# Two of eight list maxima placed between dependent folds in a top-k attention kernel

## Chip, cores and metric

The kernel runs on one core of a Trainium2 chip. The metric is the time of one execution in microseconds of the device; the median of three runs of the kernel before is 854.37 us (853.60 to 854.74). The profile is one further execution with a span of 853.3 us.

## The reference

Attention that keeps, in each row of scores, only those not below the row's 32nd largest, followed by a highway layer on the result. Cut to what matters:

```python
# q, k, v: (8, 8, 576, 64) float32
scores = scale * np.matmul(q, k.transpose(0, 1, 3, 2))          # 576 scores a row
kth = np.partition(scores, -32, axis=-1)[..., -32:-32 + 1]
scores = np.where(scores >= kth, scores, -1000000000.0)
attn = np.exp(scores - scores.max(axis=-1, keepdims=True))
x = (attn / (attn.sum(axis=-1, keepdims=True) + 1e-09)) @ v     # to (4608, 512)
H = np.maximum(x @ w_h, 0.0)
T = 1.0 / (1.0 + np.exp(-(x @ w_t + b_t)))
out = T * H + (1.0 - T) * x
```

## The kernel before

A *tile* is 128 query rows of one head (or 64 rows of two heads). Two tiles make a *pair*, the unit of a step; two pairs make a *quad*. There are 144 steps and 72 quads, numbered from 0. A *group* is the set of pairs that share the same rows of one batch: four pairs, or two for the remainder of 64 rows.

**How the 32nd largest value of a row is found.** Sorting 576 values on VectorE in rounds of eight would be long, so the row is first split into lists by pairwise maxima and minima:

- `tree` (L250), once in a step: `hi` holds the larger of score i and score i + 288, for two tiles of the quad. It reads the scores in PSUM (`ps`) and ScalarE's copy in SBUF (`z`, written by `evac`, L239). As soon as it ends, PE may overwrite the single PSUM tile `ps` with the next pair's scores.
- `folds` (L267), once a quad, at odd steps, for all four tiles at once: `hh` is the larger of the halves of `hi` (144 values a tile), `h3` the larger of the halves of `hh` (72), and a third operation puts the smaller of those halves into columns 72 to 143 of the list `w2`. Each of the first two reads what the instruction in front of it wrote; the third reads `hh`.
- `minima` (L287) on POOL: with integer additions it turns `hh` and `hi`, in place, into the smaller ones of their pairs. It is made to wait for the last fold of the quad.
- `tops` (L312), a generator for each tile: largest eight of `h3`, strike them out, next eight, strike them out, then the largest eight of each half of the small `hh`. That is six steps of one VectorE operation each (a strike-out shows in the trace as two rows, a load of the values and the replacement).
- `rest` (L333), a generator for each tile: largest eight of the small `hi`, then the last rounds over the 168 collected values; it ends with the threshold `m4`.

VectorE's maximum of eight is MAX8 in the trace. `run` (L389) advances a list of generators in turn, one step of each a round, so that neighbouring instructions belong to different tiles:

```python
    def run(gens, rounds=99):
        while gens and rounds:
            gens[:] = [x for x in gens if next(x, 0) is None]
            rounds -= 1
```

**Order.** Engines are fed in the order of the program (`keep_in_program_order`, L35), so the order below is also that of each queue. In step n the loop at L974 issues: the tree of pair n; at odd n the folds and POOL's minima of quad n // 2 (L979); masks and the product with the values of earlier pairs on ScalarE and PE; the scores and `evac` of pair n + 1; pieces of the highway layer. Then come VectorE's lists. At odd n `rest` for the first two tiles of quad n // 2 - 1 and two rounds of `rest` for its other two (L1032). At even n the end of those two, and then all of `tops` for the four tiles of quad n // 2 - 1, in rounds; a group that has ended puts a reciprocal (`norm`) behind the second round:

```python
                    gens = ops.lists(n - 2, *pairs[n - 2]) if have(n - 2) else []
                    ops.run(gens, 2)
                if ended:
                    ops.norm(pairs[n - 5][0])
                ops.run(gens)
```

So VectorE ends an even step with eight MAX8 on `hh` of the older quad (two rounds over four tiles), and begins the odd step with tree, `hh`, `h3` and the third fold of the newer one. `settle` (L394), on POOL, subtracts the lists' ends from the threshold once a group is done.

In the profile every instruction of the main loop has the line L35, which records it, so it is told by its tiles: `hi<-ps,z` is the tree, `hh<-hi` the first fold, `h<-hh` the second, `w<-hh` as TENSOR_TENSOR the third and as MAX8 a list maximum.

Of the kernel before, what the change touches and what calls it, by code (L numbers as in the profile page):

```python
# [67 lines left out]
class Ops:  # L68
# [195 lines left out]
            hi[:, half, :], ps[:, :, 0:H1], sc[:, :, H1:S], ALU.max  # L264
        )

    def folds(self, k, g, pi):  # L267


        vec, P, S, H = self.nc.vector, self.P, self.S, self.H  # L270
        H1, H2, H3 = S // 2, S // 4, S // 8
        if pi == 0:
            g.w2 = self.lpool.tile([P, H, H2 + 32], FP32, tag="w2", name="w2")
        hi, hh, h3 = self.quads[k]
        vec.tensor_tensor(hh[:], hi[:, :, 0:H2], hi[:, :, H2:H1], ALU.max)
        a, b = hh[:, :, 0:H3], hh[:, :, H3:H2]
        vec.tensor_tensor(h3[:], a, b, ALU.max)
        last = vec.tensor_tensor(
            g.w2[:, 2 * pi : 2 * pi + 4, H3:H2], a, b, ALU.min
        )  # L280
        if k == 0:
            last = vec.tensor_tensor(
                hh[:], hi[:, :, 0:H2], hi[:, :, H2:H1], ALU.min
            )
        return last
# [478 lines left out]
def kernel(  # L764
# [65 lines left out]
    with ExitStack() as cm:  # L830
        ops = Ops(cm, tc, shared, exact=False)

        def load_weights():
            for src, dst in ((moe_w_h, wh), (moe_w_t, wt)):
                ops.nc.gpsimd.dma_start(
                    dst[:], src.rearrange("(g p) n -> p g n", p=P)
                )
            bt_bcast = bass.AP(
                tensor=moe_b_t.tensor, offset=moe_b_t.offset, ap=[[0, P], [1, dm]]
            )  # L840
            ops.nc.gpsimd.dma_start(bt[:], bt_bcast)
# [7 lines left out]
        def out_rows(g):  # L849
            if not g.rem:  # L850
                r0 = g.b * S + g.qt
                return [out[r0 : r0 + JP : J, :]]
            ends = [(g.b + i) * S for i in (0, 1)]
            return [out[r1 - R : r1, :] for r1 in ends]
# [10 lines left out]
        pairs = [(g, pi) for g in groups for pi in range(len(g.pairs))]  # L865
# [36 lines left out]
        def have(n):  # L902
            return 0 <= n < NPR
# [57 lines left out]
            vec.tensor_reduce(flag_f[:], bps[0:1, 0:P], op=ALU.max, axis=AX.X)  # L961
            vec.tensor_copy(flag[:], flag_f[:])

        late = []
        def attend(m):
            ops.mask(m, *pairs[m])
            values(m - 1)
            ops.trans(m)

        def values(m):  # L970
            g, pi = pairs[m]
            ops.av(m, g, pi, preps[g.b]["vb"])

        while step <= NPR:  # L974
            n = step
            if have(n):
                ops.tree(n)
                if n % 2:
                    ops.minima(n // 2, ops.folds(n // 2, *pairs[n - 1]))  # L979
                if n + 2 < NHP:  # L980
                    ops.turn(pr, "kin", n + 2, True)
                if NHP <= n + 1 < 2 * NHP:
                    ops.turn(pr, "qin", n + 1 - NHP, None, 1)
                if n == NHP:
                    ops.load(pr, "qin", 3, None, None, 1)
                if n == 2 * NHP:
                    ops.turn_rest(pr, 0, NHP, ("qrest",))
            if n == 5:
                load_weights()
            if have(n - 4):  # L990
                ops.mask(n - 4, *pairs[n - 4], tis=(0,))
            kind = fg = None
            nextg = None
            if ffn and (ffn[0][0] != "x" or n % 2):
                kind, fg = ffn.pop(0)
                if kind == "t" and ffn and ffn[0][0] == "x":
                    nextg = ffn.pop(0)[1]
            if have(n - 5):
                values(n - 5)
            if have(n - 4):  # L1000
                ops.mask(n - 4, *pairs[n - 4], tis=(1,))
            if have(n + 1):
                g, pi = pairs[n + 1]
                ops.scores(n + 1, g, pi, preps[g.b])
                ops.evac(n + 1)
            if kind == "x":
                ops.ffn_x(fg)
            if kind == "h":
                ops.ffn_h(fg)
                ops.ffn_r(fg)  # L1010
                ops.ffn_d(fg)
            if kind == "t":
                ops.ffn_t(fg)
                ops.ffn_e(fg)
                ops.ffn_o(fg, *out_rows(fg))
            if n == 3:
                ops.values_rest(pr)
                ops.values(pr, 0)
            if n == 4:
                ops.values(pr, 1)  # L1020
            ended = False
            if have(n - 5):
                g, pi = pairs[n - 5]
                ended = pi == len(g.pairs) - 1 and (not g.rem or g.r0 > 0)
            if n % 2:
                gens = ops.lists_rest(n // 2 - 1, *pairs[n - 3]) if have(n - 3) else []
                late = gens[2:]
                gens = gens[0:2]
                if n == 1:
                    opening = ops.lists(0, *pairs[0])  # L1030
                    ops.run(opening, 2)
                ops.run(gens)  # L1032
                ops.run(late, 2)
            else:
                ops.run(late)
                if n == 2:
                    gens = opening
                else:
                    gens = ops.lists(n - 2, *pairs[n - 2]) if have(n - 2) else []
                    ops.run(gens, 2)  # L1040
                if ended:
                    ops.norm(pairs[n - 5][0])
                ops.run(gens)
            if nextg:
                ops.ffn_x(nextg)
            if have(n - 4):
                ops.trans(n - 4)
            if ended and not pairs[n - 5][0].last:
                ops.norm_heads(pairs[n - 5][0])
            for piece in pieces.pop(n, []):  # L1050
                piece()
            if n % 2 == 0 and have(n - 3):
                g, pi = pairs[n - 3]
                if pi == len(g.pairs) - 1:
                    ops.settle(g)
            if ended:
                g = pairs[n - 5][0]
                ffn += [("x", g), ("h", g), ("t", g)]
            step += 1
# [13 lines left out]
        late = ops.lists_rest(m // 2 + 1, *pairs[m + 1])  # L1073
        gens, late = late[0:2], late[2:]
# [49 lines left out]
    with tc.If(taken > 0):  # L1124
        with tc.For_i(0, B, 1) as b:
            with ExitStack() as cm:
                ops = Ops(cm, tc, shared, exact=True)
# [17 lines left out]
                n = 0  # L1145
                for qt in range(nck):
                    g = Group(b, qt, 0, H, P)
# [49 lines left out]
```

## Time and profile before

| | |
|---|---|
| median of three runs | 854.37 us |
| span of the profiled execution | 853.3 us |
| VectorE (DVE) busy | 823.3 us, 96% |
| ScalarE (ACT) busy | 762.4 us, 89% |
| GpSimd (POOL) busy | 710.4 us, 83% |
| TensorE (PE) busy | 706.0 us, 83% |
| tree: count, median | 142, 737 ns |
| fold `hh`: count, median | 73, 758 ns |
| fold `h3`: count, median | 72, 457 ns |
| third fold: count, median | 72, 451 ns |
| MAX8 on `hh` (72 values): count, median | 576, 217 ns |

[...] neighbours on one engine can overlap, so starts, and not durations, add up to the span. Busy time counts an overlap once. The trees of the first two pairs and one more fold of quad 0 have forms of their own.

### The profile page before, as it was taken

To read this page: it belongs to the slowest core of one execution; us is meant where nothing else is said; L and a number is where in the kernel's file an instruction comes from. 1 tells how busy PE (TensorE), PEld (TensorE's weight loads), DVE (VectorE), ACT (ScalarE), POOL (GpSimd) and SP (SyncE) were. 2 spreads that over 40 slices of the span, in tenths; PEclk is the share of its full clock that TensorE was granted. 3 is DMA by queue.
4 is the path that set the end of the run, shared out by engine and by line. 5 is a ranking of instruction groups with operands and counts; after the bars stand their busy time and mean duration, and the time that the engine had idled before them with its cause. 6 is when DMAs were issued, how large, how long until landed. Compare 5 with 4: busy or idle time off the path is not lost.

```text
span 853.3 us, 20051 instructions
## 1 busy us (share of the span) xinstructions
PE 706.0 (83%) x6520; PEld 492.0 (58%) x6566; DVE 823.3 (96%) x4168; ACT 762.4 (89%) x1523; POOL 710.4 (83%) x457
## 2 busy tenths in 40 slices
PE   7788888888888888888888888879888888887865
PEld 4565555565566555565556555656556665555543
DVE  4999999999999999999999999999999999999994
ACT  3799998899999999799999999989999999889974
POOL 5788888888889889878889888888888988887991
PEclk9699999999999999999999999999999999999998
DMA  8463413234244331433325342323413211111311
GB/s 187 126 114 69 112 33 68 51 70 99 38 90 91 75 88 27 74 70 63 88 51 94 64 108 41 63 50 69 112 39 68 49 34 28 39 38 26 47 33 38
DMA packets 105184, 58.12 MB, mean 68 GB/s; under 512 B 82288, under 2 KB 91888, under 8 KB 105072
## 3 DMA queue, kind: packets, MB, share of 16 engines
q1 hardware_dynamic: 93200, 37.47, 17.1%
q0 software_dynamic: 11056, 19.01, 15.7%
q8 instruction: 53, 0.87, 0.4%
q14 instruction: 59, 0.48, 0.2%
q10 hardware_dynamic: 816, 0.30, 0.1%
HBM read 30.67 MB, written 18.35 MB: 57 GB/s over the span
## 4 chain that ended last, share of the span: by engine, by line
DVE 92%; PE 3%; ACT 2%; POOL 1%; issue 1%; DVEq 0%; POOLq 0%; ACTq 0%
DVE w L35 50%; DVE m L35 19%; DVE hi L35 11%; DVE hh L35 7%; DVE h L35 4%; PE ps L35 1%; ACT pen L35 1%; ACT et L35 1%; PE t L35 1%; PE kqps L35 0%; DVE scales L35 0%; PE zt L35 0%; ACT z L35 0%; POOL hh L35 0%; PE warm L35 0%
## 5 line engine op out<-in xcount | busy, mean ns | idle before, releaser
L35 PE MATMUL ps<-kq 64*128 64x64 f32 (+3 forms) x1280 | 210.6, 453 | 65.4 <-DVE hi L35 62.6
L35 ACT ACTIVATE pen<-z,m 128x576 bf16<-128x576 f32 x288 | 226.7, 788 | 0.2
L35 PE MATMUL zt<-ident,z 128*128 128x128 f32 x1152 | 217.3, 282 | 5.5 <-ACT xT L35 5.5
L35 ACT ACTIVATE z<-ps 128x1152 f32<-128x1152 f32 x144 | 162.9, 1131 | 58.7 <-PE ps L35 56.2
L35 PE MATMUL zt<-nident,pen 128*128 128x128 bf16 x1152 | 207.5, 221 | 0.1
L35 PEld LDWEIGHTS ps<-kq 64*128 64x128 f32 (+1 forms) x1280 | 106.7, 182 | 164.2 <-issue 83.6
L35 POOL TENSOR_TENSOR hi<-z,hi 128x1152 int32<-128x1152 int32 x72 | 189.3, 2629 | 13.9 <-DVE m L35 8.3
L35 POOL TENSOR_TENSOR hi<-hi,z 128x1152 int32<-128x1152 int32 x72 | 190.5, 2646 | 5.6
L35 PEld LDWEIGHTS zt<-ident,z 128*128 128x128 f32 x1152 | 164.4, 143 | 21.4 <-ACT xT L35 6.4
L35 POOL TENSOR_TENSOR hh<-hi,hh 128x576 int32<-128x576 int32 x71 | 104.0, 1465 | 87.2 <-DVE w L35 87.2
L35 ACT ACTIVATE et<-zt 128x512 bf16<-128x512 f32 x288 | 163.6, 601 | 9.4 <-PE zt L35 4.9
L35 PEld LDWEIGHTS <-pen 128*128 128x128 bf16 x1440 | 152.8, 107 | 14.4 <-ACT pen L35 9.1
L35 DVE MAX8 m<-w 128x8 f32<-128x168 f32 x576 | 159.7, 318 | 0.0
L35 PE MATMUL zr<-v,et 128*128 128x65 bf16 (+1 forms) x1590 | 98.3, 196 | 45.4 <-ACT et L35 38.1
L35 PEld LDWEIGHTS <-et 128*128 128x128 bf16 (+1 forms) x1600 | 69.2, 101 | 84.2 <-ACT et L35 81.7
L35 DVE MAX8 w<-hi 128x8 f32<-128x288 f32 x288 | 116.1, 444 | 0.0
L35 DVE TENSOR_TENSOR hi<-ps,z 128x576 f32<-128x576 f32 x142 | 104.7, 737 | 1.3 <-ACT z L35 1.2
L35 POOL TENSOR_TENSOR hh<-hh,hi 128x576 int32<-128x576 int32 x71 | 100.2, 1411 | 5.6
L35 DVE MATCH_REPLACE8 w<-m,w 128x168 f32<-128x168 f32 x288 | 89.0, 316 | 0.0
L35 DVE MAX8 w<-hh 128x8 f32<-128x72 f32 x576 | 84.0, 217 | 0.0
L35 PE MATMUL zr<-ident,z 128*128 128x128 f32 x286 | 68.9, 294 | 6.0 <-ACT xs L35 5.9
L35 ACT ACTIVATE x<-xs,scales 128x64 f32<-128x64 f32 x272 | 68.2, 336 | 0.0
(96 smaller groups left out, 1154.3 us busy)
## 6 DMA issues: line engine op xcount, KB each, us to landing
x<-d POOLq DMA_DIRECT2D x34, 256.0 KB, 3.9
vin<-in_v_dram SPq DMA_DIRECT2D x8, 1024.0 KB, 5.6
kin<-in_k_dram SPq DMA_DIRECT2D x63, 128.0 KB, 3.2
out_dram<-d SPq DMA_DIRECT2D x30, 256.0 KB, 2.2
out_dram<-t POOLq DMA_DIRECT2D x30, 256.0 KB, 4.1
qin<-in_q_dram SPq DMA_DIRECT2D x56, 128.0 KB, 3.0
qrest<-in_q_dram SPq DMA_DIRECT2D x8, 128.0 KB, 4.1
vrest<-in_v_dram SPq DMA_DIRECT2D x8, 128.0 KB, 2.9
```

Of the source, the lines that this page charges most:

```text
L35: return self._tc.keep_in_program_order(fn(*args, **kw))
```

## The change

`folds` is given a list of up to two generators. It advances the first to its end ahead of the fold `hh` and the second ahead of the fold `h3`. At even steps the loop runs `tops` for three more rounds, after which each of the four tiles has one MAX8 left; those of the first two tiles follow as before, and those of the other two are kept in `fill` for the folds of the next step. In the last step, which no folds follow, all four run at once.

```diff
-    def folds(self, k, g, pi):
+    def folds(self, k, g, pi, fill):
...
         hi, hh, h3 = self.quads[k]
+        self.run(fill[0:1])
         vec.tensor_tensor(hh[:], hi[:, :, 0:H2], hi[:, :, H2:H1], ALU.max)
+        self.run(fill[1:2])
         a, b = hh[:, :, 0:H3], hh[:, :, H3:H2]
         vec.tensor_tensor(h3[:], a, b, ALU.max)
...
-        late = []
+        late, fill = [], []
...
                 if n % 2:
-                    ops.minima(n // 2, ops.folds(n // 2, *pairs[n - 1]))
+                    ops.minima(n // 2, ops.folds(n // 2, *pairs[n - 1], fill))
+                    fill = []
...
                 if ended:
                     ops.norm(pairs[n - 5][0])
+                ops.run(gens, 3)
+                if have(n + 1):
+                    gens, fill = gens[0:2], gens[2:4]
                 ops.run(gens)
```

## The prediction

> **What bounds the kernel now.** I read the page's shares first, then the windows, then the chain of waits. In the first fence (the page) the busy shares leave VectorE ahead, and the chain runs over it for nine tenths of the span.
>
> ```profile
> span 853.3 us, 20051 instructions
> ...
> PE 706.0 (83%) x6520; PEld 492.0 (58%) x6566; DVE 823.3 (96%) x4168; ACT 762.4 (89%) x1523; POOL 710.4 (83%) x457
> ...
> DVE 92%; PE 3%; ACT 2%; POOL 1%; issue 1%; DVEq 0%; POOLq 0%; ACTq 0%
> ```
>
> 96% is an average over a start and a tail in which VectorE has little to do. The windows view (each engine's busy time in a stretch) for the middle of the run has:
>
> ```profile
> 63.00:700.00 637.00, 538.79 (x5056) 377.23 (x5094) 633.13 (x3228) 595.57 (x1198) 549.41 (x343) 0.99 0.34 68
> ```
>
> Columns: stretch, length, then PE, PEld, DVE, ACT, POOL. DVE is busy 633.13 of 637.00 us (99.4%). ScalarE is next with 595.57 (93.5%), which is the room that a faster VectorE finds before it meets another bound. So VectorE's own queue, instruction after instruction, is the kernel; but "busy" says nothing of how tightly its instructions follow one another. That is in the timeline (start, us, engine, operation). One step pair of VectorE, around the folds:
>
> ```profile
> 402.35 0.56 DVE L35 MAX8 m<-w 128x8 f32<-128x168 f32 x2
> 402.82 0.74 DVE L35 TENSOR_TENSOR hi<-ps,z 128x576 f32<-128x576 f32 x1
> 403.47 0.08 DVE L35 MATCH_VALUE_LOAD w<-m,w 128x8 f32 x1
> ...
> 407.31 1.17 DVE L35 MAX8 w<-hh 128x8 f32<-128x72 f32 x8
> 408.40 0.73 DVE L35 TENSOR_TENSOR hi<-ps,z 128x576 f32<-128x576 f32 x1
> 409.17 0.76 DVE L35 TENSOR_TENSOR hh<-hi 128x576 f32<-128x576 f32 x1
> 409.96 0.46 DVE L35 TENSOR_TENSOR h<-hh 128x288 f32<-128x288 f32 x1
> 410.34 0.45 DVE L35 TENSOR_TENSOR w<-hh 128x288 f32<-128x288 f32 x1
> 410.71 0.81 DVE L35 MAX8 w<-hi 128x8 f32<-128x288 f32 x2
> ```
>
> Read starts, not durations. Where an instruction needs nothing of the one in front of it, it starts about 0.08 us before that one ends: the tree of 402.82 lasts 0.74, and the next starts 0.65 later. Where it reads the result just written, it starts after the end: tree to hh is 409.17 - 408.40 = 0.77, hh to h3 is 0.79. Two such places stand in every quad.
>
> [...] a 72-wide maximum lasts 217 ns in its row but starts follow at (408.40 - 407.31) / 8 = 0.136 us, 0.08 less. [...] a start 0.03 after the end instead of 0.08 before it is the cost of reading the neighbour's result[...]. [...] the overlap at 402.82 shows that a switch from a PSUM reader to an SBUF reader isn't held.
>
> **The change part by part.** *What moves.* No instruction is added or removed; no wait is added. Of the eight MAX8 on hh that stand ahead of the odd tree, two go behind it, one on either side of the hh fold. On PE, ACT, POOL and SP the order of instructions is what it was, so no DMA is moved past anything. This happens in quads 1 to 71, 71 times (VectorE's listed rows grow by 142 only because the run of eight is broken up).
>
> *Cost per quad, before.* Eight maxima at 0.136 = 1.09, tree to hh 0.77, hh to h3 0.79: 2.65.
>
> *After.* Six maxima, 0.82. Tree to the first held maximum 0.65 (the 402.82 pair), then 0.136 until the hh fold could start: 0.79. The fold's operand is ready at 0.77, as now, so the maximum, not the wait, sets the start, by 0.02. The hh fold to the second maximum: the fold's 0.76 less 0.08 = 0.68, plus 0.136 = 0.81, against readiness at 0.79. Sum 0.82 + 0.79 + 0.81 = 2.42. **Gain 0.23 us a quad**: of two maxima that cost 0.272, all but 0.04 lies in time that is now latency.
>
> *How many count.* The chain of waits leaves VectorE for good with the even tree at 812.14, the last but one. Folds of quads 1 to 70 lie ahead of it: 70 x 0.23 = 16.1 us. Quad 71's fold lies in the tail, where PE and ACT work carry the chain; I count nothing, at most 0.23.
>
> *What it loses.* The odd tree now comes two maxima (0.27) earlier and needs ScalarE's copy of the scores (z). Usually that waits: in the ScalarE timeline z ends at 407.39 for the tree at 408.40 and at 417.69 for 419.68, 1 to 2 us early. But the odd tree at 22.57 already waits for its z (ends 22.53), so moving maxima behind it gains nothing there: quad 1 loses 0.27. The one at 45.28 has 0.13 of room (z ends 45.15): 0.14 lost. Six more trees have 0.3 to 0.4 (z ends 248.96, tree 249.32); there I take off 0.1 each, a choice: they have the room for one quad's 0.27, not for two. Sum 1.0, net 15.1.
>
> *What else moves with it.* POOL's minima are released by the last fold, which comes 0.23 earlier, so POOL keeps its place relative to VectorE. The maxima read hh of the quad before, whose POOL work ended at 412.36 + 1.41 = 413.77 where the maxima start at 418.59, so they meet no wait. POOL's settle, which reads the lists, is queued after the closing maxima of the same quad, which follow the folds in both orders: no cost. PE's scores wait for the tree (62.6 us in all), which comes earlier.
>
> *Unknown costs.* A fold two places behind its producer with only a 0.136 maximum between isn't in the trace. Nearest is 400.08, two 168-wide maxima, then a load of the first one's result:
>
> ```profile
> 400.08 0.56 DVE L35 MAX8 m<-w 128x8 f32<-128x168 f32 x2
> 400.55 0.07 DVE L35 MATCH_VALUE_LOAD w<-m,w 128x8 f32 x1
> ```
>
> The second maximum ends at 400.64, and the load starts at 400.55: the wait is for the producer alone, and the neighbour still overlaps. There readiness has 0.1 to spare, here 0.02. Lower bound of the cost: nothing beyond the above (the maximum sits in the queue anyway). Upper, by the wait's own overhead (0.03) not being hidden: 0.03 at 142 places, 4.3 us. I take nothing, and keep 4.3 for the range. Below nothing: POOL's doubled output DMAs stretch a few folds (the hh row has a maximum of 1054 ns against a median of 758); other phases could spare or add some 1.5 us in all.
>
> Against the span: 853.3 - 15.1 = 838.2. The three timed runs have a median of 854.37, 1.1 above this span; so the time is 854.37 - 15.1 = 839.3, rounded to **839.2**.
>
> **The rivals.** *ScalarE takes over.* Speaking for it: 93.5% busy, and several quads in which it never idles. Against: 595.57 us over 637 / 11.28 = 56.5 quads is 10.5 a quad against 11.05 after the change, and it still waits 56.2 us for PE's scores. If its work had bursts that took half the gain: 854.4 - 8 = 846.4.
>
> *The change doesn't do what it says.* If the hh fold waited for the maximum too, each link would be 0.65 + 0.217 + 0.03 = 0.90, which is what 0.136 + 0.77 is now (h3: 0.68 + 0.25 = 0.93, as 0.136 + 0.79). Exactly nothing gained: 854.4. The pair at 400.08 speaks against it.
>
> *Slower.* One mechanism: at the boundary of a fold and a small maximum, neither side overlaps[...]. Then a link is 0.74 + 0.03 + 0.217 + 0.03 = 1.02 instead of 0.90, 0.12 lost twice in 71 quads: +17 us, 871. It begins to decide where an inserted maximum costs more than 0.116 beyond its hidden place. For it: the trace has no maximum between these folds. Against: last maximum to tree (407.31 to 408.40) and w fold to maximum (410.34 to 410.71) both overlap by 0.08.
>
> **How the numbers follow.** The forecast has 0.86, ScalarE's bursts 0.07, no effect 0.03, slower 0.04. The forecast's own range is 854.37 - 16.4 - 1.5 = 836.5 up to 839.2 + 4.3 = 843.5. It holds over 8 in 10, with little of the second case; I stop at 844. A measurement of this kernel tells 0.2% (1.7 us) from no change: faster 0.93, same 0.03, slower 0.04.
>
> **What would show it.** Right: in the timeline after, six maxima together, then tree, maximum, hh, maximum, h3, with starts 0.65, 0.14, 0.68, 0.14 apart, no idle time ahead of hh or h3, quads of 11.05 us from hh to hh instead of 11.28 (409.17 to 420.45), and DVE busy time nearly unchanged while the span falls (less overlap lost, not less work). Links of 0.82 or more behind the tree mean that the wait isn't wholly hidden; of 0.90, that the fold waits for the maximum. DVE waits on ACT for z beyond some 2 us in sum would show the second case. The forecast is wrong if the quad period falls by less than 0.15.

## The result and the profile after

The changed kernel's median is 839.76 us (837.78 to 842.48) beside 853.99 for the one before in the same comparison: ratio 0.9838, 95% interval 0.9807 to 0.9870. In a second, larger comparison further down it is 841.61 beside 852.67: 0.9861, 0.9840 to 0.9881. Faster, by 11 to 14 us; the forecast was 839.2 with a range of 836.5 to 844.

From the page after, the span, the busy times and the chain's shares:

```profile
span 837.7 us, 20051 instructions
...
PE 699.8 (84%) x6520; PEld 488.8 (58%) x6566; DVE 812.2 (97%) x4168; ACT 761.3 (91%) x1523; POOL 712.0 (85%) x457
...
DVE 82%; ACT 7%; PE 5%; POOL 2%; issue 2%; SPq 1%; DMA 0%; DVEq 0%; ACTq 0%; POOLq 0%
```

DVE's busy time has fallen too, from 823.3 to 812.2 us, with the same instructions: busy time counts an overlap once, and there is more overlap. I had expected it nearly unchanged, and that could not be: VectorE's idle time ahead of the two folds was only 5.0 us before (2.5 each), so most of the gain had to come out of busy time. The chain leaves VectorE for longer than before; one such stretch, on ScalarE and PE from about 752 to 780 us, ends in a wait that is taken up below. The windows view of the stretch that the prediction used:

```profile
63.00:700.00 637.00, 546.65 (x5173) 383.42 (x5209) 636.68 (x3300) 606.30 (x1218) 561.01 (x350) 0.99 0.34 69
```

VectorE now passes 3300 counted instructions in 637 us instead of 3228, and is busy all but 0.3 us of them. ScalarE has 606.30, 95.2%: still second, with less room. The timeline of VectorE after, around one set of folds:

```profile
409.33 0.90 DVE L35 MAX8 w<-hh 128x8 f32<-128x72 f32 x6
410.15 0.74 DVE L35 TENSOR_TENSOR hi<-ps,z 128x576 f32<-128x576 f32 x1
410.80 0.23 DVE L35 MAX8 w<-hh 128x8 f32<-128x72 f32 x1
410.94 0.74 DVE L35 TENSOR_TENSOR hh<-hi 128x576 f32<-128x576 f32 x1
411.60 0.23 DVE L35 MAX8 w<-hh 128x8 f32<-128x72 f32 x1
411.75 0.44 DVE L35 TENSOR_TENSOR h<-hh 128x288 f32<-128x288 f32 x1
412.11 0.45 DVE L35 TENSOR_TENSOR w<-hh 128x288 f32<-128x288 f32 x1
```

Read the starts: tree to maximum 0.65, maximum to hh 0.14, hh to maximum 0.66, maximum to h3 0.15, h3 to the third fold 0.36. Each fold starts 0.08 before the maximum in front of it ends (411.60 + 0.23 = 411.83 against 411.75); nothing waits any more. From hh at 399.90 to hh at 410.94 a quad takes 11.04 us where it took 11.28.

The tree's rows of before and after, in this order, as the view of the tile hi gives them (minimum, median, maximum duration in ns, then first and last start):

```profile
L35 DVE TENSOR_TENSOR hi<-ps,z x142: 728/737/758, 18.2 to 817.6; 128x576 f32<-128x576 f32 x142
```

```profile
L35 DVE TENSOR_TENSOR hi<-ps,z x142: 727/734/758, 16.4 to 802.5; 128x576 f32<-128x576 f32 x142
```

From the third tree to the last it took 799.4 us and takes 786.1: 13.3 less. The other 2.3 of the two spans' difference of 15.6 are not from the loop: 1.8 lies ahead of the third tree and 0.5 behind the last. In the second profile of the changed kernel that tree starts at 18.3, so the 1.8 is how one start differs from another. In what follows I compare this stretch, "tree to tree", as well as times.

### The profile page after: what moved, and what is told of

Read it like the earlier page. It is cut to its first block, busy times and chain, and to the rows that moved or that the text cites. A ratio compares the mean times of both kernels' runs of the same rounds, so it can differ in the third digit from the quotient of the medians.

```text
span 837.7 us, 20051 instructions
## 1 busy us (share of the span) xinstructions
PE 699.8 (84%) x6520; PEld 488.8 (58%) x6566; DVE 812.2 (97%) x4168; ACT 761.3 (91%) x1523; POOL 712.0 (85%) x457
## 3 DMA queue, kind: packets, MB, share of 16 engines
q0 software_dynamic: 11056, 19.01, 15.6%
## 4 chain that ended last, share of the span: by engine, by line
DVE 82%; ACT 7%; PE 5%; POOL 2%; issue 2%; SPq 1%; DMA 0%; DVEq 0%; ACTq 0%; POOLq 0%
DVE w L35 45%; DVE m L35 18%; DVE hi L35 10%; DVE hh L35 5%; DVE h L35 3%; PE ps L35 2%; PE zt L35 2%; ACT z L35 2%; ACT pen L35 2%; ACT x L35 1%; ACT et L35 1%; POOL hh L35 1%; POOL hi L35 1%; PE zr L35 1%; PE t L35 1%
## 5 line engine op out<-in xcount | busy, mean ns | idle before, releaser
L35 PE MATMUL ps<-kq 64*128 64x64 f32 (+3 forms) x1280 | 206.6, 446 | 48.8 <-DVE hi L35 45.8
L35 PEld LDWEIGHTS ps<-kq 64*128 64x128 f32 (+1 forms) x1280 | 104.8, 179 | 144.0 <-issue 81.8
L35 DVE MAX8 w<-hh 128x8 f32<-128x72 f32 x576 | 96.3, 216 | 0.0
```

Source lines behind the costliest of these rows:

```text
L35: return self._tc.keep_in_program_order(fn(*args, **kw))
```

## The experiments

**One maximum, ahead of hh alone.** Here and in the next kernel a single tile is held back.

```diff
-        self.run(fill[1:2])
-                    gens, fill = gens[0:2], gens[2:4]
+                    gens, fill = gens[0:3], gens[3:4]
```

> One list maximum a quad is held back and put ahead of the hh fold; the fold h3 follows hh directly as before. Theory A (each inserted maximum fills the latency of its own link): half of the gain, 0.12 us x 70 = 8.4 of DVE time, about 846 us; in the timeline tree to hh is about 0.80 with the maximum between, hh to h3 0.79 as before. Rival B (the gain comes from the tree being issued earlier, by which PE, ScalarE and POOL are released earlier): the tree comes one maximum earlier, also about half, 847; B alone would leave the links' sum unchanged.

Measured: 844.70 beside 853.42, ratio 0.9901 (0.9875 to 0.9926); tree to tree 791.9.

**One maximum, ahead of h3 alone.**

```diff
-        self.run(fill[0:1])
         vec.tensor_tensor(hh[:], hi[:, :, 0:H2], hi[:, :, H2:H1], ALU.max)
-        self.run(fill[1:2])
+        self.run(fill[0:1])
-                    gens, fill = gens[0:2], gens[2:4]
+                    gens, fill = gens[0:3], gens[3:4]
```

> One list maximum a quad is held back and put ahead of the h3 fold; the hh fold follows the tree directly as before. Theory A: 0.125 us x 70 = 8.7, about 845.5 us; tree to hh 0.77 as before, hh to h3 about 0.80 with the maximum between. Rival B: as with the one ahead of hh, 847. If one of the two links gave no gain, this run and the one ahead of hh would differ by some 8 us.

Measured: 845.65, ratio 0.9908 (0.9887 to 0.9929); tree to tree 791.8. The two links give the same, 7.5 and 7.6 us between the trees. Together that would be 15.1, and the change has 13.3: the halves do not quite add up. The one wait of 1.76 us near 780 us, which neither half has and which is taken up below, is as large as what is missing.

**The same maxima behind the folds.** This has the earlier tree without the filled links.

```diff
-        self.run(fill[0:1])
         vec.tensor_tensor(hh[:], hi[:, :, 0:H2], hi[:, :, H2:H1], ALU.max)
-        self.run(fill[1:2])
...
             g.w2[:, 2 * pi : 2 * pi + 4, H3:H2], a, b, ALU.min
         )
+        self.run(fill)
```

> The same two maxima are held back, but put behind the third fold: the tree comes two maxima earlier as in the change, and the folds stand next to each other as before. Theory A: no link is filled, no gain, 854 us within 2. Rival B (the earlier tree makes the gain): about 840 us, as with the change. This is the run that tells the two apart.

Measured: 855.21, ratio 1.0017 (1.0004 to 1.0029); tree to tree 800.2. The timeline of VectorE in this kernel:

```profile
406.57 0.91 DVE L35 MAX8 w<-hh 128x8 f32<-128x72 f32 x6
407.39 0.74 DVE L35 TENSOR_TENSOR hi<-ps,z 128x576 f32<-128x576 f32 x1
408.17 0.76 DVE L35 TENSOR_TENSOR hh<-hi 128x576 f32<-128x576 f32 x1
408.96 0.46 DVE L35 TENSOR_TENSOR h<-hh 128x288 f32<-128x288 f32 x1
409.33 0.45 DVE L35 TENSOR_TENSOR w<-hh 128x288 f32<-128x288 f32 x1
409.70 0.36 DVE L35 MAX8 w<-hh 128x8 f32<-128x72 f32 x2
```

The tree stands where the change has it, the links are 0.78 and 0.79 as before, and there is no gain at all. An earlier release of PE, ScalarE or POOL is worth nothing here; rival B falls.

**Both maxima ahead of hh.**

```diff
-        self.run(fill[0:1])
+        self.run(fill[0:2])
         vec.tensor_tensor(hh[:], hi[:, :, 0:H2], hi[:, :, H2:H1], ALU.max)
-        self.run(fill[1:2])
```

> Both held maxima stand ahead of the hh fold, none ahead of h3. Theory A: the first fills the link, the second finds nothing left to fill: tree to hh 0.65 + 0.14 + 0.14 = 0.93, hh to h3 0.79; gain 0.12 a quad, about 846 us, the same as one maximum ahead of hh. Rival C (what counts is how many maxima lie behind the tree): about 840 us, as with the change.

Measured: 846.94, ratio 0.9918 (0.9894 to 0.9941); tree to tree 791.8, the same as with one maximum there. Starts of tree, hh and h3 in its timeline are 404.43, 405.36 and 406.13: 0.93 and 0.77. The second maximum pays its full 0.136. So it matters in which link a maximum stands, not how many lie behind the tree.

**The dependence removed instead of filled.** From the kernel before; h3 is formed from the hh of the quad before instead of its own, and the flag for the exact pass is held at zero.

```diff
-        vec.tensor_tensor(h3[:], a, b, ALU.max)
+        old = self.quads[k - 1][1] if k else hh
+        vec.tensor_tensor(h3[:], old[:, :, 0:H3], old[:, :, H3:H2], ALU.max)
...
-            vec.tensor_copy(flag[:], flag_f[:])
+            vec.tensor_scalar(flag[:], flag_f[:], 0.0, None, ALU.mult)
```

> The kernel before, with one dependence taken away instead of filled: the fold h3 reads the hh tile of the quad before, so that it does not need what the instruction in front of it wrote (h3 and with it the thresholds are then wrong ones; the flag for the second, exact pass is set to zero; the amount of work is the same). Theory A: hh to h3 falls from 0.79 to 0.66 or 0.68 with nothing between, 0.12 x 71 = 8.5 us, about 845.5 us, equal to the run with one maximum ahead of h3. If the 0.79 were the fold's own pace and not a wait for its operand, nothing changes: 854 us.

Measured: 846.18 beside 852.67, ratio 0.9920 (0.9902 to 0.9938). Its timeline of VectorE:

```profile
403.63 0.76 DVE L35 TENSOR_TENSOR hh<-hi 128x576 f32<-128x576 f32 x1
404.30 0.45 DVE L35 TENSOR_TENSOR h<-hh 128x288 f32<-128x288 f32 x1
404.67 0.45 DVE L35 TENSOR_TENSOR w<-hh 128x288 f32<-128x288 f32 x1
```

hh to h3 is 0.67 instead of 0.79, with nothing between. The 0.12 belongs to the dependence and not to the fold; this is its cost by itself. The third fold is now the first to need this hh, with h3 in between, and it starts 0.08 before h3 ends (404.67 against 404.75): with its producer two places back, needing a result cost nothing here.

**All four last maxima, two in each link.**

```diff
+        self.run(fill[0:2])
         vec.tensor_tensor(hh[:], hi[:, :, 0:H2], hi[:, :, H2:H1], ALU.max)
+        self.run(fill[2:4])
...
-                    gens, fill = gens[0:2], gens[2:4]
+                    gens, fill = [], gens
```

> All four last maxima of a quad are held back, two ahead of hh and two ahead of h3. Theory A: the latency of a link is filled by one maximum already; a second can only take away the 0.01 us that a link has left behind its maximum (0.143 and 0.146 from the maximum to the fold instead of 0.135), 0.019 x 70 = 1.3 us at most: 838 to 840 us. If more latency were left, it would be clearly faster than the change, 830 or below. Against it: the tree now comes four maxima earlier and may wait for ScalarE's copy of the scores more often, 1 to 2 us.

Measured: 845.05, ratio 0.9895 (0.9877 to 0.9912), while the changed kernel beside it had 841.61. This was a miss: I had expected 838 to 840. VectorE and, in the second fence, POOL in the timeline of this kernel:

```profile
403.30 0.73 DVE L35 TENSOR_TENSOR hi<-ps,z 128x576 f32<-128x576 f32 x1
403.95 0.35 DVE L35 MAX8 w<-hh 128x8 f32<-128x72 f32 x2
404.23 0.89 DVE L35 TENSOR_TENSOR hh<-hi 128x576 f32<-128x576 f32 x1
```

```profile
403.23 1.27 POOL L35 TENSOR_TENSOR t<-t,x 128x512 f32<-128x512 f32 x1
404.80 0.88 POOL L35 DMA_DIRECT2D out_dram<-t  x1 [0.30 <-POOL t L35]
```

The fold lasts 0.89 instead of 0.74: POOL's multiplication of the highway layer runs until 404.50, 0.27 into it, and the run without the multiplication, below, tests this. Of 14 folds seen in the timeline of this kernel six last 0.89 to 0.91. POOL's chain starts at the third fold of the quad before; with four maxima behind the tree hh begins earlier still in that chain. The group rows of hh in this kernel and of the changed one show the mean grow from 770 to 822 ns, 52 x 73 = 3.8 us in all. With 2.1 us more of waiting for z (5.9 instead of 3.8 in the trees' group row) that is about the 5.7 us by which it is longer tree to tree (791.8 against 786.1):

```profile
L35 DVE TENSOR_TENSOR hh<-hi 128x576 f32<-128x576 f32 x73 | 60.0, 822 | 0.1
```

```profile
L35 DVE TENSOR_TENSOR hh<-hi 128x576 f32<-128x576 f32 x73 | 56.2, 770 | 0.1
```

**Without POOL's multiplication.** The product t by x is left out, from the changed kernel (twice) and from the one before.

```diff
-            self.nc.gpsimd.tensor_tensor(g.t[:], g.t[:], g.x[:], ALU.mult)
```

> The changed kernel without POOL's multiplication of t by x in the highway layer (that product is left out, 1.27 us of POOL a group). Theory D: the hh fold[...], is stretched where that multiplication runs beside it (0.74 to 1.33 us at three places in the changed kernel's profile, 0.76 to 1.05 in the one before): without it all hh folds last 0.74 to 0.78, and the time falls by some 2 us against the changed kernel, to about 838. Rival: the stretch comes from the output DMAs that POOL issues next; then the 1.33 stay.

> The kernel before without POOL's multiplication of t by x (that product is left out). The changed kernel without it took 833.3 us, some 7 to 8 less than with it, of which the trace shows about 3.5 between the first and the last tree and 3.4 in the tail, where the product stood on the path. In the kernel before only 4 hh folds meet the multiplication, in the changed one 32. Theory D: here the part between the trees is smaller, about 2 us, the tail is the same 3.4, so about 848 us, and the change without the multiplication is worth 15 us or more, against 11 to 14 with it. Rival: the multiplication costs both kernels the same 7 to 8, then 845.5.

> The changed kernel without the multiplication once more, beside the one above on the same chip: 833 us within 1. Theory D: 15 us or more below the kernel before without it; rival: 12 below.

Measured: from the changed kernel 833.28 (ratio 0.9763, 0.9745 to 0.9781) and again 833.85; from the one before 849.55 beside 853.77 (0.9952, 0.9936 to 0.9967). The view of the tile hh in the first of them has no long fold left:

```profile
L35 DVE TENSOR_TENSOR hh<-hi x73: 726/734/771, 14.2 to 800.9; 128x576 f32<-128x576 f32 x73
```

Its maximum is 771 ns; in the changed kernel it is 1332. So the stretch is the multiplication and not the DMAs that follow it. Tree to tree is 796.9 before and 782.6 after: the change is worth 14.3 us there without the multiplication (14.7 with the first of the two profiles, 782.2) and 13.3 with it. In the whole time it is worth 849.55 - 833.85 = 15.7, against 11 to 14. From the changed kernel 8.3 us came off (833.28 beside 841.61), and not the 2 that I had expected: 3.5 to 3.9 of it between the trees. Most of the rest is the tail: from the last tree to the end of the span both kernels take 31.8 us without the multiplication, instead of 35.2 after the change and 35.7 before it, since the last multiplication stands on the path there (from 813.28, for 1.28 us, in the chain after the change).

**The changed kernel again.**

> The changed kernel again, for a closer time and a second profile. In the first profile VectorE waited once for 1.76 us for the scores' copy near 780 us, where TensorE's granted clock had fallen to half for 3.4 us and the scores took 2.40 instead of 1.30 us. If that is chance (theory), the second profile has such stretches at other places, the quads are again 11.03 to 11.12 us long, and the time is 838 to 841 us; if the change causes it, the wait is there again.

Measured: 841.61, ratio 0.9861 (0.9840 to 0.9881); span 839.3, tree to tree 18.3 to 804.4, again 786.1. But the wait near 780 is there again, 1.47 us behind scores of 2.11 us. My theory of chance falls. From the first profile, PE, and then VectorE, near that place:

```profile
776.63 2.40 PE L35 MATMUL ps<-kq 64*128 64x512 f32 x8
```

```profile
780.24 0.76 DVE L35 TENSOR_TENSOR hi<-ps,z 128x576 f32<-128x576 f32 x1 [1.76 <-ACT z L35]
```

The same scores took 1.30 us in the kernel before. Two windows of 3.41 us of the changed kernel, ahead of the slow scores and from their start on (the third number from the end is the granted clock):

```profile
773.17:776.58 3.41, 1.31 (x18) 1.05 (x18) 3.41 (x22) 3.15 (x7) 3.33 (x2) 1.00 0.00 0
776.58:779.99 3.41, 3.08 (x14) 1.62 (x12) 1.90 (x17) 2.14 (x4) 3.11 (x3) 0.50 0.02 5
```

The clock is at half through the whole of the second, 3.41 us; in the first it was full, and PE was busy for 1.31 us only. All profiles with both links filled have long scores at this step: 2.40 and 2.11 us in the two of the changed kernel, 2.40 with two maxima in each link, 2.40 and 2.13 without the multiplication. How busy PE was just ahead does not settle it. In the kernel before it was busy for 1.75 of the 3.41 us ahead of the same scores, and the clock stayed full; in the changed one the clock fell at 278.23 and at 479.62 behind 1.91 and 1.92. Why it fell at this step in the five profiles and not in that of the kernel before was not tried and stays open.

The slow scores are not the whole of the wait. They took 1.10 us longer and VectorE waited 1.76; in the second profile it is 0.81 and 1.47. Both times 0.66 is left. That part fits ScalarE, which the chain runs over in this stretch and which is busy here for 18.68 of 19.00 us (fourth in the list of engines; 18.28 at the corresponding place before):

```profile
756.40:775.40 19.00, 14.87 (x149) 10.35 (x148) 18.96 (x89) 18.68 (x42) 14.40 (x8) 1.00 0.12 29
```

That it is ScalarE's work is my reading of these two figures; no run tried it by itself.

## Why the prediction was right

**The mechanism held at each step.** Tree to maximum 0.65 (forecast 0.65), maximum to hh 0.14 (0.14), hh to maximum 0.66 (0.68), maximum to h3 0.15 (0.14). The fold waits for its producer alone and overlaps the maximum, although readiness has only 0.02 to spare; the upper bound of 0.03 a place wasn't needed. The run that puts the maxima behind the folds excludes the earlier tree as the cause, and the one without the dependence measures the latency by itself.

**The gain per quad was a little undersized.** 0.23 was forecast and 0.25 is measured (11.28 to 11.03 or 11.04). The missing 0.02 is in the folds: I took their durations from the rows of before, where they stood right behind the tree or another fold. The rows of before and of after, from the view of the tile hh:

```profile
L35 DVE TENSOR_TENSOR h<-hh x72: 457/457/460, 15.3 to 819.2; 128x288 f32<-128x288 f32 x72
```

```profile
L35 DVE TENSOR_TENSOR h<-hh x72: 428/434/458, 13.5 to 804.1; 128x288 f32<-128x288 f32 x72
```

h3 falls from 457 to 434 ns and hh from 758 to 741. So what follows them starts 0.02 earlier: hh to the maximum 0.66, h3 to the third fold 0.36 instead of 0.38. The open wait is not the main reason: in the run without the dependence h3 waits for nothing, still stands behind hh, and keeps a median of 451. So what shortens h3 is mostly the maximum in front of it. The row of the run without the dependence:

```profile
L35 DVE TENSOR_TENSOR h<-hh x72: 445/451/525, 13.7 to 811.2; 128x288 f32<-128x288 f32 x72
```

**The losses were undersized by more.** 70 quads at 0.25 are 17.5 us; the trees show 13.3, so 4.2 were lost where I took off 1.0. The first part is the term I had, the waits for z. The tree's group row of before and of after (idle time in front of it last):

```profile
L35 DVE TENSOR_TENSOR hi<-ps,z 128x576 f32<-128x576 f32 x142 | 104.7, 737 | 1.3 <-ACT z L35 1.2
```

```profile
L35 DVE TENSOR_TENSOR hi<-ps,z 128x576 f32<-128x576 f32 x142 | 104.4, 735 | 3.8 <-ACT z L35 3.3
```

That is 2.5 us more, and 1.76 of it is the one place near 780: 1.10 from the halved clock, which I had not thought of, and 0.66 that fits ScalarE. Of the six tight trees that I had put at 0.1 each, three lost 0.2 each: 0.11 of idle time and the 0.08 by which they would have overlapped the maximum in front. The second part, about 1.0, was missing from my sum: the folds' meeting with POOL's multiplication. I had seen the long fold of 1054 ns, put it down to POOL's output DMAs, and taken it at nothing with some 1.5 us for the range; the runs without the multiplication show that the cause was another. Mean less median, times 73, is (774 - 758) x 73 = 1.2 us before and (770 - 741) x 73 = 2.1 after for hh; and taking the multiplication away raises the gain from 13.3 to 14.3. I had written that POOL "keeps its place relative to VectorE". It keeps its place to the third fold of the quad before; the next hh comes 0.24 earlier in that chain. In the kernel before 4 hh folds run beside the multiplication, after the change 32, most of them by 0.12 to 0.16 us with little or no harm (these last 0.73 to 0.78). Of the 0.7 that is left of the 4.2, some 0.5 is the overlap that each of the six newly waiting trees loses besides its idle time; about 0.2 I can't allot.

So there is luck in how closely the forecast of 839.2 met the first measurement: its terms have 1.4 too little gain against 3.2 too little loss, which would leave it at 841.0; the second measurement is 841.6.

**The rivals.** That ScalarE takes over didn't come for the kernel as a whole, but its sign did: I had named waits on ACT for z beyond some 2 us, and they are 3.3 in all. 1.2 of them were there before and 1.10 stand behind the slow scores; the rest, most of it near 780, is a small piece of this rival. That the fold waits for the maximum, and that neither side overlaps, are excluded by the timeline. No run here was slower than the kernel before except the one with the maxima behind the folds, by 0.04 to 0.29%, at the edge of what can be told.

## What to carry to other kernels

On an engine that is busy all the time, as VectorE is here, look at the starts of neighbours: where an instruction reads what the one in front of it wrote, an independent one between them was nearly free, once for each such link: two of 0.136 us took 0.02 together. One of 0.136 us was long enough; a shorter one was not tried. A second one in the same link paid its full price. Then ask what the other engines do at the moment to which the work was moved: here a quarter of the gain was given back, to a POOL operation that held up folds and to waits that the shorter steps opened.

## What the runs showed of the hardware

**A dependence between neighbours cost 0.12 us on VectorE** between these folds, as 0.08 of lost overlap and 0.03 from end to start. One 72-wide maximum, 0.136 from start to start, hid all of it. Behind a maximum the folds' own rows were also 0.02 shorter (741 against 758 ns, 434 against 457), for the most part not by the dependence: without it, behind a fold, it is 451.

**A POOL operation held folds.** The longest case in the changed kernel, VectorE and then POOL:

```profile
255.19 1.33 DVE L35 TENSOR_TENSOR hh<-hi 128x576 f32<-128x576 f32 x1
```

```profile
254.64 1.27 POOL L35 TENSOR_TENSOR t<-t,x 128x512 f32<-128x512 f32 x1
```

The fold's row starts at 255.19, POOL ends at 255.91, and the fold ends 0.61 later, at 256.52. So it is with all ten folds of the kernel before (four) and of the changed one (six) that meet the multiplication for over 0.2 us: each ends 0.61 or 0.62 us behind it. The stretch of 0.59 (1.33 - 0.74) is the overlap of 0.72 less 0.13; folds of the changed kernel that meet the multiplication for 0.125 us or less last 0.73 to 0.75, no longer than others. The prediction left the multiplication out. The tree (`hi<-ps,z`) ran beside it without a stretch: in the changed kernel 32 trees meet it for 0.48 us or more and last 0.73 to 0.76 (one is 399.10, 0.73, with POOL's from 398.77 to 400.04). Why it held the fold and not the tree was not tried.

**TensorE's clock was halved for 3.41 us at a time in the middle of busy stretches**, and the scores that fell into one near 780 us took 2.40 instead of 1.30 us and held up VectorE through ScalarE. The kernel before has such stretches too (scores of 2.39 us at 812.85, without a wait behind them). From 60 to 800 us the clock fell six times in the profile of the kernel before and five times in the first of the changed one, each time for 3.41 us. In the 3.41 us just ahead PE had been busy for 1.23 to 1.92 us. Of the 420 other stretches of that length in the two profiles six were below 2.0 us as well (1.88 to 1.99), with no fall behind them.
